# Two-bank PSUM tiles at the end of batch 0, and a later start of batch 1's last DFT, in a fused FFT-mixing and MLP kernel

## The chip, the cores and the metric

The kernel runs on one core of a Trainium2 chip. The metric is the time of one execution on the device in microseconds. The kernel before takes 848.44 us (median of 3 runs, 848.11 to 849.39). The granted clock of TensorE (the share of its full speed that it is let run at) is given.

## The reference

For each of 8 batches of 3008 x 256 values: an FFT along the sequence, a complex 256 x 256 product with bias, a soft threshold, the inverse FFT; then a two-layer MLP with a squared ReLU over all 24064 rows.

```python
X = np.fft.rfft(x, axis=1)
Yr = Xr @ w_r - Xi @ w_i + b_r          # and Yi likewise
Yr = np.sign(Yr) * np.maximum(np.abs(Yr) - 0.01, 0.0)
y  = np.fft.irfft(Yr + 1j * Yi, n=3008, axis=1)

r = np.maximum(y @ w_in, 0.0)           # 256 -> 2048, "hidden"
out = (s * (r * r) + b) @ w_out         # 2048 -> 256, "output"
```

As `(s*r*r + b) @ w_out = s*(r*r) @ w_out + b * colsum(w_out)`, the kernel computes the column sum of w_out once.

## The kernel before

The FFT of length 3008 = 94 x 32 is done in steps: an input DFT over 94 (result `u`), a forward DFT over 32, the mixing product, an inverse DFT over 32 (`v`), and a last DFT over 94 (result `yt`). Batch 0 keeps all of this on the chip; its `v` is turned by identity matmuls (`vt` to `vs`). Later batches go through DRAM (`ud`, `vd`), and their pieces are spread over slots of the MLP's main loop. A slot is one chunk `mc` of hidden units; there are 16 to a tile of up to 512 columns.

The kernel uses eight banks of PSUM, the memory that matmuls write to. `psa` (`other_bank`) and `psf` (`one_bank`) have two each. The other four are `psm` during batch 0 and then `psh`, two tiles of two banks, for the hidden matmuls.

```python
def any_bank():                       # batch 0's tail rotates through all eight
    turn_of[0] += 1
    if "h" in pools:
        return (other_bank, one_bank)[turn_of[0] % 2]()
    return (mix_bank, one_bank, mix_bank, other_bank)[turn_of[0] % 4]()

def turn(ec, k):                      # in first_batch()
    for i in range(2):
        ps = any_bank() if ec else mix_bank()
        ...                           # 4 matmuls into the bank
        evac(vs[...], ps[0:96]..., 512)

def last_dft(ec, n2):
    if ec or n2 >= 16:
        ps = [any_bank(), any_bank()]
    else:
        ps = [one_bank(), other_bank()]
    ...                               # 8 matmuls, 4 into each bank
    for i in range(2):
        evac(yt[...], ps[i][:, 0:384]..., 384)
...
for k in range(4):
    turn(1, k)
    some(1)                           # one unit of batch 1's input DFT
    if k:
        last_dft(1, 8 * (k - 1))
last_dft(1, 24)
```

`evac` gives a PSUM tile to ScalarE or VectorE, whichever has less estimated load. The column sum of w_out is made by GpSimd (`sum_w_out`, eight adds), then spread over the partitions by one matmul of ones, planned for slot 15:

```python
def make_bias():
    ps = other_bank()
    nc.tensor.matmul(ps[:, 0:D], ones, w_sum, start=True, stop=True)
    for j in range(2):
        nc.scalar.activation(out=bias_bc[:, j], in_=ps[:, 0:D], func=AF.Copy, scale=bb_bc)
...
schedule(0, 10, more)
plan.setdefault(15, []).append(make_bias)
...
schedule(mark[1] - 14, 12, s4_units(1))   # batch 1's last DFT: 14 units over 12 slots
```

The order in which the program is written is not the order on the engines: the framework's scheduler lays the instructions out per engine when the program is built. An engine's list is then worked off in order: in the changed kernel, below, TensorE stands 1.53 us before one matmul while ready ones are next in its list.

## Time and profile before

| what | value |
|---|---|
| time | 848.44 us; span in the profile 846.2 us |
| TensorE, VectorE, ScalarE busy | 99%, 82%, 76% |
| first hidden matmul, first ReLU of the MLP | 47.94 us, 49.14 us |
| 6th, 41st, 49th ReLU of the MLP | 54.56, 129.73, 147.74 us |
| batch 1's last DFT | begins at 130.88 us |

The starts of the MLP's ReLUs are used below as milestones: there are 384 in every version, so the n-th in one trace answers to the n-th in another, and the difference of their starts tells how late one kernel is at that point.

### The profile page before, as it was taken

Reading aid. Unit: us, or ns where it says so; the run is one execution under the profiler, and the core shown is the slowest. Engines: PE = TensorE matmul, PEld = TensorE weight load, DVE = VectorE, ACT = ScalarE, POOL = GpSimd, SP = SyncE. Lnnn points to the kernel's source line nnn. Section 1 sums busy time; section 2 is a strip of 40 time slices with the busy share of each in tenths; the row PEclk is TensorE's granted clock in tenths of the full one; section 3 lists DMA queues with packets and bytes.
Section 4 is the critical chain, followed back from the end, with each engine's and each line's share of the span. In section 5 each row is a group of like instructions: output and inputs, shape, how many; then the busy total and the mean of one; then the engine's idle time right before and its main releaser. Section 6 shows DMA issues by size and latency. Waiting matters only on the chain.

```text
span 846.2 us, 17115 instructions
## 1 busy us (share of the span) xinstructions
PE 833.9 (99%) x6653; PEld 599.6 (71%) x6653; DVE 691.8 (82%) x1026; ACT 642.7 (76%) x864; POOL 46.0 (5%) x71
## 2 busy tenths in 40 slices
PE   8999999999999999999999999999999999999997
PEld 6857766777677766777677776777667777766765
DVE  5989987888878987888888888798977888776674
ACT  5988886787778787788777887788877778666673
POOL 4341000000000001000000000000000000000000
PEclk9999999999999999999999999999999999999999
DMA  8945568224762367324761247613354223411111
GB/s 201 181 142 122 122 151 212 67 72 103 173 185 57 99 169 182 96 75 108 189 170 51 78 102 199 171 41 91 101 156 122 62 78 97 112 33 38 38 44 50
DMA packets 105747, 96.06 MB, mean 114 GB/s; under 512 B 9543, under 2 KB 97483, under 8 KB 104323
## 3 DMA queue, kind: packets, MB, share of 16 engines
q1 hardware_dynamic: 99218, 80.55, 32.9%
q0 software_dynamic: 6448, 14.42, 10.7%
q8 instruction: 52, 0.85, 0.4%
q14 instruction: 29, 0.23, 0.1%
HBM read 53.52 MB, written 46.66 MB: 118 GB/s over the span
## 4 chain that ended last, share of the span: by engine, by line
PE 89%; DVE 4%; DMA 3%; ACT 3%; issue 1%; POOL 0%; DVEq 0%; ACTq 0%; SPq 0%; POOLq 0%
PE psa L840 36%; PE psh L769 36%; PE psf L635 4%; PE psf L570 2%; PE psf L621 2%; PE psf L606 2%; PE psf L718 2%; PE psf L665 2%; ACT rt L776 1%; DVE gt L783 1%; DMA vd<-v 1%; PE psm L426 1%; DMA vs<-vd 1%; DMA x<-in_x_dram 1%; DMA F_c<-dft_fwd 0%
## 5 line engine op out<-in xcount | busy, mean ns | idle before, releaser
L776 ACT ACTIVATE rt<-psh 128x1024 f32<-128x1024 f32 (+2 forms) x384 | 386.8, 1009 | 119.6 <-PE psh L769 117.8
L783 DVE TENSOR_TENSOR gt<-rt 128x1024 f16<-128x1024 f32 (+2 forms) x321 | 383.9, 1199 | 98.3 <-ACT rt L776 97.6
L840 PE MATMUL psa<-w_out_t,gt 128*128 128x256 f16 (+1 forms) x3024 | 454.6, 272 | 0.1
L840 PEld LDWEIGHTS <-gt 128*128 128x128 f16 (+1 forms) x3024 | 301.0, 101 | 187.0 <-issue 1.4
L769 PE MATMUL psh<-yt,w_in 128*128 128x512 f16 (+1 forms) x1344 | 396.3, 378 | 0.2 <-ACT rt L776 0.2
L769 PEld LDWEIGHTS <-w_in 128*128 128x128 f16 x1536 | 142.9, 98 | 28.0 <-issue 2.0
L850 DVE SCALAR_TENSOR_TENSOR ost<-psa,s_bc,bias_bc 128x512 f32<-128x512 f32 (+2 forms) x97 | 71.0, 732 | 8.3 <-PE psa L840 6.7
L780 ACT ACTIVATE gt<-rt 128x1024 f16<-128x1024 f32 (+2 forms) x63 | 66.2, 1050 | 1.0
L640 DVE TENSOR_TENSOR ring<-psf,s 128x512 f16<-128x512 f32 x84 | 57.4, 684 | 3.7 <-PE psf L635 3.1
L170 ACT CAST v<-psf 128x512 f16<-128x512 f32 x78 | 45.3, 582 | 18.7 <-PE psf L665 18.7
L170 ACT CAST xf<-psf 128x512 f16<-128x512 f32 x82 | 47.9, 585 | 10.9 <-PE psf L606 10.8
L769 PE MATMUL psh<-tail,w_in 128*128 128x512 f16 (+1 forms) x192 | 52.1, 353 | 0.0
L170 ACT CAST u<-psf 96x512 f16<-96x512 f32 x75 | 43.4, 580 | 10.9 <-PE psf L570 10.7
L635 PE MATMUL psf<-W_g,xf 128*128 128x256 f16 x336 | 50.4, 272 | 0.0
L170 ACT CAST yt<-psf 128x480 f16<-128x480 f32 (+2 forms) x73 | 37.3, 523 | 14.2 <-PE psf L718 14.2
L213 POOL DMA_DIRECT2D x<-in_x_dram x36 | 18.7, 526 | 432.4 <-PE psf L570 431.2
L570 PE MATMUL psf<-x,A_t 94*96 94x512 f16 x103 | 39.3, 381 | 1.7 <-ACT yt L170 0.5
L646 DVE TENSOR_TENSOR ring<-ring,high 128x512 f16<-128x512 f16 x84 | 35.5, 423 | 2.3
L647 DVE TENSOR_TENSOR ring<-ring 128x512 f16<-128x512 f16 x84 | 35.4, 422 | 1.9
L645 DVE TENSOR_TENSOR ring<-ring,low 128x512 f16<-128x512 f16 x84 | 35.4, 421 | 1.6
L635 PEld LDWEIGHTS <-xf 128*128 128x128 f16 x336 | 32.9, 98 | 3.9
L718 PE MATMUL psf<-C_t,vs 96*128 96x96 f16 x448 | 33.0, 205 | 0.9 <-DMA vs<-vd 0.8
(97 smaller groups left out, 500.7 us busy)
## 6 DMA issues: line engine op xcount, KB each, us to landing
out_dram<-ost SPq DMA_DIRECT2D x152, 128.0 KB
ud<-u SPq DMA_DIRECT2D x28, 384.0 KB
us<-ud SPq DMA_DIRECT2D x28, 384.0 KB
vd<-v SPq DMA_DIRECT2D x42, 256.0 KB
vs<-vd SPq DMA_DIRECT2D x14, 768.0 KB
x<-in_x_dram POOLq DMA_DIRECT2D x28, 376.0 KB, 6.5
ring<-ring SPq DMA_DIRECT2D x280, 32.0 KB
out_dram<-ost SPq DMA_DIRECT2D x16, 120.0 KB
```

Of the source, the lines that this page charges most:

```text
L170: return None, nc.scalar.copy(out=dst, in_=src)
L570: nc.tensor.matmul(ps[0:96, :], A_t[0:N1, :], x16[(b, c)][0:N1, j * D : (j + 2) * D], start=True, stop=True,)
L635: nc.tensor.matmul(ps[:, r, :], xt[:, 2 - r, dc], W_g[:, dc, r], start=(dc == 0), stop=(dc == DC - 1),)
L640: nc.vector.tensor_tensor(out=t, in0=ps, in1=hold[i // 2][:, i % 2].unsqueeze(1).to_broadcast([P, 2, D]), op=ALU.add,)
L646: nc.vector.tensor_tensor(out=m, in0=m, in1=high, op=ALU.min)
L718: nc.tensor.matmul(ps[:, j * 96 : (j + 1) * 96], vs[(b, h)][:, k, ec * P : (ec + 1) * P], C_t, start=True, stop=True,)
L769: nc.tensor.matmul(o, w_in_t[dc][:, mc * P : (mc + 1) * P], r, start=(dc == 0), stop=(dc == DC - 1),)
L776: nc.scalar.activation(out=rt[:, :, 0:w], in_=ps[:, :, 0:w], func=AF.Relu)
L780: nc.scalar.activation(out=gt[:, :, 0:w], in_=rt[:, :, 0:w], func=AF.Square)
L783: nc.vector.tensor_tensor(out=gt[:, :, 0:w], in0=rt[:, :, 0:w], in1=rt[:, :, 0:w], op=ALU.mult)
L840: nc.tensor.matmul(ps[0:size, h, :], gts[(ti, mc // 2)][:, mc % 2, sub * size : (sub + 1) * size], w_out_t[:, mc, :], start=(mc == 0), sto ...
L850: nc.vector.scalar_tensor_tensor(out=ost[0:size, 0:k], in0=ps[0:size, 0:k], scalar=s_bc[0:size], in1=bias_bc[0:size, 0:k], op0=ALU.mult, o ...
```

## The change

Its intent: the last four turns and six of the eight last DFTs of batch 0 fill a PSUM tile of two banks and are read by one instruction each (10 evacuations for 20); for this psm is closed and psh opened two steps before the end of batch 0's loop. Besides, batch 1's last DFT starts two slots later and is spread over 16 slots, to wait less for its reload and to have one unit to a slot.

```diff
         def turn(ec, k):
+            if ec:
+                ps = two_banks()
+                for j in range(8):
+                    nc.tensor.matmul(ps[0:96, j // 4, (j % 4) * P : (j % 4) * P + P],
+                                     vt[:, ec, 8 * k + j, :], eye_t, start=True, stop=True)
+                evac(vs[...][:, n : n + 8, ...], ps[0:96]..., 1024)
+                return
         def last_dft(ec, n2):
             if ec or n2 >= 16:
-                ps = [any_bank(), any_bank()]
-            else:
-                ps = [one_bank(), other_bank()]
+                two = two_banks()
+                ...                   # the same 8 matmuls
+                evac(yt[...], two[:, :, 0:384]..., 768)
+                return
+            ps = [one_bank(), other_bank()]
...
         for i in range(2 * U + 2):
+            if i == 2 * U:
+                mix_pool.close()
+                pools["h"] = ctx.enter_context(
+                    tc.tile_pool(name="psh", bufs=2, space=bass.MemoryType.PSUM))
...
-    schedule(mark[1] - 14, 12, s4_units(1))
+    schedule(mark[1] - 12, 16, s4_units(1))
```

(The pool psm is opened inside `first_batch`, and psh is no longer opened after it; the turns that stay single take `mix_bank` without a choice.)

More of the change, by code (lines that the diff above doesn't have):

```diff
@@ L363, in first_batch @@
     def first_batch():
+        mix_pool = ExitStack()
+        pools["m"] = mix_pool.enter_context(
+            tc.tile_pool(name="psm", bufs=4, space=bass.MemoryType.PSUM)
+        )
         ut = ypool.tile([P, DC, 96, N2], F16, name="ut", tag="yt")
@@ L486, in turn @@
         def turn(ec, k):
+            if ec:
+                ps = two_banks()
+                for j in range(8):
+                    nc.tensor.matmul(
+                        ps[0:96, j // 4, (j % 4) * P : (j % 4) * P + P],
+                        vt[:, ec, 8 * k + j, :], eye_t, start=True, stop=True,
+                    )
+                h, n = divmod(8 * k, HW)
+                evac(
+                    vs[(0, h)][:, n : n + 8, ec * P : (ec + 1) * P],
+                    ps[0:96].rearrange("p h (j e) -> p (h j) e", e=P), 1024,
+                )
+                return
             for i in range(2):
-                ps = any_bank() if ec else mix_bank()
+                ps = mix_bank()
                 n = 8 * k + 4 * i
@@ L505, in last_dft @@
             if ec or n2 >= 16:
-                ps = [any_bank(), any_bank()]
-            else:
-                ps = [one_bank(), other_bank()]
+                two = two_banks()
+                for j in range(8):
+                    h, k = divmod(n2 + j, HW)
+                    nc.tensor.matmul(
+                        two[:, j // 4, (j % 4) * 96 : (j % 4) * 96 + 96],
+                        vs[(0, h)][:, k, ec * P : (ec + 1) * P], C_t,
+                        start=True, stop=True,
+                    )
+                evac(
+                    yt[:, ec, n2 : n2 + 8, :].rearrange("p (h j) n -> p h j n", h=2),
+                    two[:, :, 0:384].rearrange("p h (j n) -> p h j n", n=96), 768,
+                )
+                return
+            ps = [one_bank(), other_bank()]
             for j in range(8):
@@ L530, in first_batch @@
         for i in range(2 * U + 2):
+            if i == 2 * U:
+                mix_pool.close()
+                pools["h"] = ctx.enter_context(
+                    tc.tile_pool(name="psh", bufs=2, space=bass.MemoryType.PSUM)
+                )
             if i < 2 * U:
@@ L865, in schedule @@
             plan.setdefault(start + (i * span) // len(units), []).append(u)
-    with tc.tile_pool(name="psm", bufs=4, space=bass.MemoryType.PSUM) as pool:
-        pools["m"] = pool
-        more = first_batch()
-    pools["h"] = ctx.enter_context(
-        tc.tile_pool(name="psh", bufs=2, space=bass.MemoryType.PSUM)
-    )
+    more = first_batch()
     load.update(act=0.0, dve=0.0)
```

## The prediction

> **What bounds the kernel now.** I read the page first, then busy time by window, the waits of TensorE, the chain that ended last in two stretches, and the timeline where the two edits act. The page's first part says that TensorE is the bound:
>
> ```profile
> PE 833.9 (99%) x6653; PEld 599.6 (71%) x6653; DVE 691.8 (82%) x1026; ACT 642.7 (76%) x864; POOL 46.0 (5%) x71
> ```
>
> Only 846.2 - 833.9 = 12.3 us of the span have no matmul in flight, and both edits touch short stages, so nothing here can be worth 2% (17 us). The question is what those two stages lose. Windows (stretch, its length, then busy us and count of PE, PEld, DVE, ACT, POOL, then clock, DMA share, GB/s):
>
> ```profile
> 37.40:41.90 4.50, 3.85 (x45) 2.61 (x43) 4.50 (x9) 3.98 (x9) 0.85 (x1) 1.00 0.67 97
> 41.90:46.20 4.30, 3.55 (x56) 2.79 (x54) 4.30 (x9) 4.26 (x10) 3.99 (x5) 1.00 0.60 176
> 46.20:49.14 2.94, 2.61 (x15) 1.31 (x15) 2.20 (x4) 2.00 (x4) 2.78 (x3) 1.00 0.00 0
> ```
>
> This is the end of batch 0, which the first edit rewrites (37.4 is where its last DFT of n2 16 begins, 49.14 the first Relu of the second network). Until 46.2 VectorE has no gap and ScalarE almost none: it is bound by evacuations, not by TensorE. From 46.2 to 49.14 neither is full. The chain that ended last (start, us, what) and the timeline agree:
>
> ```profile
> 39.08 0.93 DVE yt L174 x2
> 40.00 0.60 DVE u L174
> ...
> 44.36 0.49 ACT u L170
> 44.84 0.49 ACT vs L170
> ```
>
> ```profile
> 47.27 0.56 DVE L174 CAST yt<-psm 128x384 f16<-128x384 f32 x1 [0.61 <-PE psm L511]
> 47.73 0.38 PE L570 MATMUL psf<-x,A_t 94*96 94x512 f16 x1 [0.28 <-ACT u L170]
> 47.74 1.27 DVE L174 CAST u<-psa 96x512 f16<-96x512 f32 x2
> 47.80 1.54 PEld L769 LDWEIGHTS <-w_in 128*128 128x128 f16 x8 [0.60 <-POOL acc L344]
> 47.94 1.89 PE L769 MATMUL psh<-yt,w_in 128*128 128x512 f16 x8
> ```
>
> The chain gives the true pace of an evacuation in a full queue (start to start): 0.60 us for 512 columns on VectorE, 0.49 on ScalarE. The timeline shows the hand-over: the last psm bank is read until 47.83, and the first matmul into psh, which takes over the psm banks, starts at 47.94. The second edit's stage, in the chain:
>
> ```profile
> 124.04 6.79 DMA vs<-vd
> 130.84 0.05 issue
> 130.88 0.60 PE psf L718 x10
> ...
> 137.28 0.42 PE psh L769 x2
> 137.70 0.06 issue
> 137.76 0.66 DVE yt L174
> 138.43 0.04 issue
> 138.47 0.37 PE psf L718 x5
> 138.84 0.41 PE psh L769 x2
> ```
>
> Batch 1's last DFT asks for vs about 0.75 us before the reload lands (TensorE's list of waits puts 0.8 us on it, once), and later TensorE stands for a psf bank until a VectorE evacuation ends.
>
> **What the Trainium skill says.** "Perfetto Trace Analysis", section Optimizing Scalar/DVE Operations, puts the overhead of an instruction that reads PSUM at about 125 ns on VectorE and 51 ns on ScalarE, and says that larger operations help a saturated engine, while splitting them can finish work sooner on one that isn't. Here two widths give the overhead: VectorE pitches of 0.60 (512 columns) and 0.465 (384, half of the 0.93 above) have a slope of 1.05 ns per column and leave 0.06 us; ScalarE's 0.49 and 0.38 leave about 0.05. ScalarE agrees with the page; VectorE's is half the page's. "Advanced Engine Details and Errata", section The Read-Write Bubble, says that one instruction may read several PSUM banks; the trace has it (Relu of 128x1024 out of psh, mean 1009 ns). "Perfetto Trace Analysis", section Matmul Optimizations, wants all eight banks in use. The kernel before rotates through all eight singly in this stretch, and the change keeps eight but as two pairs and four singles. "DMA: Bandwidth & Descriptors", section Rules for kernel authors: wait late on a transfer issued early. The trace agrees with its 0.8 us.
>
> **The change part by part.**
>
> *Fewer evacuations.* Six calls of the last DFT and four of the turn had two evacuations each, 20 in all; they get 10. Columns stay the same, so 10 overheads of some 0.055 us go: 0.55 us over two engines that share the work, 0.28 us of time if both stay full.
>
> *Hand-over of the banks.* In the kernel before psh can open only when psm has been read out, as the timeline shows. In the new one psh opens at step 12, in the stream: the first pair of hidden matmuls needs only the psh pair of the next-to-last DFT tile, the second pair that of the last. So hidden matmuls may start while the last tile is still read. From 46.2 to 49.14 there are 2.94 x 2 = 5.9 us of engine time, with 4.2 used: up to 0.8 us per engine to gain.
>
> *Price of pairs.* A pair takes 8 matmuls of some 0.055 us (0.44), some 0.2 us until the evacuation begins, then 0.9 to 1.13 us for 1024 columns (Relu and square in a full queue: 0.92 and 1.13) or 0.7 to 0.87 for 768 (by the slopes), then some 0.1. A cycle is 1.75 or 1.5 us on average. Four turns and four DFTs of the second half through two pairs take (4 x 1.75 + 4 x 1.5) / 2 = 6.5 us. They begin at 41.3 (first turn, which waits for the last vt), so the hidden matmuls come at about 47.6 and the first Relu at about 48.6, against 49.14. Evacuation work in the same time: 4 x 1.02 + 4 x 0.78 + 10 u tiles x 0.54 = 12.6 us, 6.3 per engine: nearly full too, so an u tile in front of a needed pair costs some tenths. I take a gain of 0.5 us for all three together; the formula alone would allow 0.9.
>
> *Last DFT of batch 1, two slots later over 16.* A slot is 0.41 + 0.44 = 0.85 us of hidden and output matmuls; start moves from slot 82 to 84, 1.7 us plus an input-DFT matmul of 0.22. The reload still lands at about 130.85, TensorE asks at about 132: the 0.75 us go. Before, 14 units over 12 slots put two in one slot twice. The first pair of units follows the wait and takes 0.60 us for ten matmuls where two fives take 0.42 (0.21 each in the chain): 0.17 lost. The second pair is the stop at 137.70: 1.14 us until 138.84 where 0.43 would do, 0.71 lost. Over 16 slots each slot has one at most. The other single slots show no loss (0.21 + 0.41 + 0.44 = 1.06 and the pitch is 1.06). So 0.75 + 0.17 + 0.71 = 1.6 us; I take 1.4, since which engine evacuates what shifts. Batch 1's first hidden tile (slot 96) needs n2 0 to 15, whose last unit is then in slot 92, so finishing at slot 98 costs nothing.
>
> Sum: 848.4 - 0.5 - 1.4 = 846.5.
>
> **Rivals.** (1) Pairs starve TensorE: with two psh pairs and in-order queues the chain turn, evacuation, DFT, evacuation gets longer, since one engine now takes 1.0 us where two took 0.6 side by side; u tiles have only psf and psa, which the last inverse DFT uses too. For it: the 6.3 against 6.5 us above leave no room. Against it: turns run one ahead of DFTs, so the latency is mostly covered. It would turn -0.5 into +1: about 848. (2) The delay is given back: u, xf and v work after slot 98 meets the last units, or the reload lands later because the start of the kernel changed. The page's busy shares of VectorE in 130 to 146 (about 75%) speak against it. It would leave -0.7: about 847.2. (3) The first stage's gain is swallowed in the first hidden tile, where no output matmuls lie beside it and ScalarE is busy 10.45 of 10.86 us (49.14 to 60.00): total evacuation work sets its end, so only the 0.28 us and the filled gaps count. About 846.9. (4) Both work in full: -0.9 and -1.6, 845.9.
>
> **Range and chances.** Between (4) with a little luck in the later balance of the two engines and (1) lies 845.0 to 848.3; three runs of before spread over 1.3 us. A move of 17 us either way has nothing to come from: faster 0.01, same 0.98, slower 0.01.
>
> **What would show it.** Right: 10 fewer evacuations in all; first Relu of the second network at about 48.6; no wait of the last DFT's matmuls on vs; no evacuation of yt in the chain in the stretch of batch 1's last DFT. Wrong: TensorE waiting on evacuations of vs between 41 and 48 and a first Relu later than 49.2, or the vs wait still there. The time would also be off if the steady stage after 150 us, which I take as unchanged, moved by over a microsecond.

## More of the kernel before

The profile's lines are shown in the prediction. Two more belong to them, which I had in view and passed over. They are from the timeline (start us, length us, engine, line, operation, out<-in, count):

```profile
49.67 0.72 POOL L345 TENSOR_TENSOR w_sum<-acc 128x256 f16<-128x256 f32 x1
...
51.99 0.27 PE L349 MATMUL psa<-w_sum,ones 128*128 128x256 f16 x1
```

GpSimd ends the column sum at 50.39. The bias matmul that needs it comes at 51.99, behind sixteen hidden matmuls, and waits for nothing.

## The result

The changed kernel takes 851.50 us (median of 6 runs, 851.18 to 853.2) against 848.68 us for the kernel before in the same rounds (847.46 to 850.08). A ratio here and below goes by mean times of runs of the same rounds, so it is not quite the ratio of the medians. It is 1.0036, with a 95% interval of 1.0023 to 1.0050: slower, by a sixth of the 2% that would count as slower. The prediction of 846.5, range 845.0 to 848.3, was wrong, and in sign.

The profiled run takes 851.18 us, with a span of 849.2 us against 846.2. The page's first line has the ten missing evacuations (VectorE 1026 to 1021, ScalarE 864 to 859), and nothing else of note:

```profile
PE 836.7 (99%) x6653; PEld 601.8 (71%) x6653; DVE 693.5 (82%) x1021; ACT 642.7 (76%) x859; POOL 48.1 (6%) x71
```

The milestones say where the time came from. The first ReLU of the MLP starts at 52.95 us against 49.14; the 17th at 79.41 against 75.25, so 4.16 late; the 41st at 133.89 against 129.73, still 4.16; the 49th at 150.53 against 147.74, 2.79 late. Some 4.2 us are lost before the second tile, 1.37 are won in the stretch of batch 1's last DFT, and nearly nothing moves after that.

The chain that ended last (followed back from the last instruction, at each step to what released it; start, us, what), for the changed kernel where the loss arises:

```profile
47.53 1.16 POOL acc L344
48.70 0.07 issue
48.76 1.17 POOL acc L344
49.93 0.07 issue
50.00 0.73 POOL w_sum L345
50.73 0.04 issue
50.77 0.37 PE psa L349
51.14 3.24 PE psh L802 x8
```

Where the chain of before has evacuations, this one holds GpSimd's adds for the column sum of w_out, and then the bias matmul. The timeline of TensorE shows the same from its side:

```profile
48.73 0.51 PE L526 MATMUL psh<-C_t,vs 96*128 96x96 f16 x8 [0.82 <-ACT vs L170]
...
50.77 0.37 PE L349 MATMUL psa<-w_sum,ones 128*128 128x256 f16 x1 [1.53 <-POOL w_sum L345]
```

The bias matmul (L349) now stands **in front of** the hidden matmuls in TensorE's list, and TensorE stands 1.53 us until the sum is there. The first hidden matmul starts at 50.94 instead of 47.94. And it doesn't run at full pace: eight hidden matmuls take 3.24 us in the chain, 0.405 each, where the chain of before has 1.94 us for eight, at most 0.24 each. Windows (stretch, length, busy us and count of PE, PEld, DVE, ACT, POOL, then granted clock, DMA share, GB/s) show why. Before:

```profile
47.00:50.70 3.70, 3.26 (x19) 1.44 (x17) 2.25 (x4) 3.19 (x5) 3.16 (x4) 1.00 0.35 102
50.70:52.00 1.30, 1.30 (x8) 0.53 (x7) 1.30 (x2) 1.30 (x3) 0.00 (x0) 1.00 0.03 13
52.00:54.50 2.50, 2.46 (x15) 1.29 (x14) 2.50 (x3) 2.50 (x4) 0.00 (x0) 1.00 0.53 157
```

After:

```profile
47.00:50.70 3.70, 1.33 (x17) 0.77 (x17) 2.04 (x3) 2.86 (x5) 3.46 (x4) 0.99 0.37 110
50.70:52.00 1.30, 1.23 (x4) 0.55 (x4) 0.00 (x0) 0.82 (x2) 0.02 (x1) 0.50 0.93 268
52.00:54.50 2.50, 2.50 (x8) 0.91 (x7) 0.50 (x1) 1.14 (x3) 0.00 (x0) 0.59 0.12 35
```

After a stretch of 3.70 us in which TensorE was busy for only 1.33, its granted clock is 0.50 and then 0.59, and the PE column reads 95 and 100% busy on half as many matmuls.

One thing more lies in the traces' clock records, and it explains oddities below. The granted clock changes only at the ends of equal stretches of 3.41 us, whose place differs from run to run. In the changed kernel's run the half clock fills one such stretch, 50.63 to 54.05; in those of experiments 3, 4 and 6 it fills two (6.83 us). Cut along these stretches, TensorE is busy in the one before the fall for 1.11 us (stretch, length, PE alone, clock, DMA share, GB/s):

```profile
47.22:50.63 3.41, 1.11 (x15) 1.00 0.39 115
50.63:54.05 3.42, 3.28 (x9) 0.50 0.39 115
```

Another stretch of this run, 9.67 to 13.09, has the half clock too. So a run's mean granted clock alone doesn't say where clock was lost.

The second part did what it was made for. The chain after, in the stretch of batch 1's last DFT, has neither the DMA nor the evacuation of `yt`; single groups of five matmuls lie between hidden and output matmuls:

```profile
138.09 0.44 PE psa L873 x4
138.53 0.21 PE psf L751 x5
138.74 0.41 PE psh L802 x2
139.15 0.44 PE psa L873 x4
```

So the theory: **the pairs of banks did not slow the evacuations much; they changed the order on TensorE, so that a matmul with a late operand came to stand in front of work that was ready, and the idleness that followed cost the clock as well.** The rivals: that pairs starve TensorE by themselves (the prediction's first rival); that a wait of ScalarE for a `u` buffer, seen below, is the cause; and that the clock fell for a reason of its own.

### The profile page after: what moved, and what is told of

Same layout as the page of the kernel before. It is cut to its first block, busy times and chain, and to the rows that moved or that the text cites. A ratio compares the mean times of both kernels' runs of the same rounds, so it can differ in the third digit from the quotient of the medians.

```text
span 849.2 us, 17102 instructions
## 1 busy us (share of the span) xinstructions
PE 836.7 (99%) x6653; PEld 601.8 (71%) x6653; DVE 693.5 (82%) x1021; ACT 642.7 (76%) x859; POOL 48.1 (6%) x71
## 4 chain that ended last, share of the span: by engine, by line
PE 90%; DMA 4%; ACT 2%; POOL 2%; issue 1%; DVE 1%; SPq 0%; DVEq 0%; ACTq 0%; POOLq 0%
PE psh L802 37%; PE psa L873 37%; PE psf L668 4%; PE psf L603 2%; DMA w_out_t<-in_moe_w_out_dram 2%; PE psf L654 2%; PE psf L639 2%; PE psf L698 2%; PE psf L751 2%; ACT rt L809 1%; POOL acc L344 1%; DMA x<-in_x_dram 1%; POOL x L213 0%; DMA F_t<-fwd_rest 0%; DVE gt L816 0%
## 5 line engine op out<-in xcount | busy, mean ns | idle before, releaser
L802 PE MATMUL psh<-yt,w_in 128*128 128x512 f16 (+1 forms) x1344 | 398.0, 379 | 0.3 <-ACT rt L809 0.2
L802 PEld LDWEIGHTS <-w_in 128*128 128x128 f16 x1536 | 143.3, 98 | 29.3 <-issue 4.7
L813 ACT ACTIVATE gt<-rt 128x1024 f16<-128x1024 f32 (+2 forms) x62 | 65.3, 1054 | 1.0
L170 ACT CAST u<-psf 96x512 f16<-96x512 f32 x79 | 45.7, 580 | 13.0 <-PE psf L603 11.7
L802 PE MATMUL psh<-tail,w_in 128*128 128x512 f16 (+1 forms) x192 | 52.1, 353 | 0.0
```

The source lines that it names most:

```text
L170: return None, nc.scalar.copy(out=dst, in_=src)
L802: nc.tensor.matmul(o, w_in_t[dc][:, mc * P : (mc + 1) * P], r, start=(dc == 0), stop=(dc == DC - 1),)
L813: nc.scalar.activation(out=gt[:, :, 0:w], in_=rt[:, :, 0:w], func=AF.Square)
```

## The experiments

Twelve kernels ran, all with correct results, five or six runs each. The kernel before had, in the rounds, medians of 848.12 (first four), 848.36 (next four) and 848.05 us (last four). Lines of the kernel files shift between versions: the hidden matmul is L769 before, L802 after, L773 or L813 below.

### 1. The change with the bias matmul held behind the hidden ones

```diff
-    plan.setdefault(15, []).append(make_bias)
+    def late_bias():
+        with tc.issue_after(hidden[(0, 7)].ins):   # the 16th hidden matmul
+            make_bias()
+    plan.setdefault(15, []).append(late_bias)
```

`issue_after` only orders the list of the engine; it is no wait.

> The changed kernel with one edge added: the bias matmul (the column sum of w_out) may be issued only after the 16th hidden matmul, where it stood before. My theory, that this matmul at the head of TensorE's queue holds the hidden matmuls back until GpSimd's sum is ready and that the idle time then halves the granted clock, expects the first Relu of the second network at about 50.5 us instead of 52.95, a clock of 1.00 between 50.7 and 54.5 instead of 0.50 to 0.59, and a time of some 848.6 us, level with the kernel before. The rival, that the pairs of banks alone starve TensorE, expects no change: 851.5 us and a low clock still.

Measured: 848.08 us (848.01 to 848.93), ratio 1.0000 (0.9988 to 1.0011). The loss against before is gone with one edge of order. (It is not at 0.9987, where experiment 2 is; see experiment 9.) The first ReLU comes at 49.26, earlier than I expected, and the 6th at 54.55, level with before (54.56). The clock stays:

```profile
47.00:50.70 3.70, 3.12 (x22) 1.39 (x20) 2.09 (x4) 3.02 (x5) 3.46 (x4) 1.00 0.66 196
50.70:52.00 1.30, 1.30 (x8) 0.58 (x6) 1.30 (x2) 1.05 (x2) 0.09 (x1) 1.00 0.13 47
```

### 2. The kernel before with the second edit alone

```diff
-    schedule(mark[1] - 14, 12, s4_units(1))
+    schedule(mark[1] - 12, 16, s4_units(1))
```

> The kernel before with the second edit alone (batch 1's last DFT from two slots later, over 16 slots). The traces of before and after differ by 1.4 us less after this stage than ahead of it, so if that is this edit's doing it gives 847.3 us, 0.9984 of before, and no wait of the last DFT on vs. The rival, that the reload only came in time because the changed kernel was late at its start, expects the wait still there and no gain: 848.7.

Measured: 847.33 us (846.87 to 847.83), ratio 0.9987 (0.9974 to 1.0000). TensorE has no wait on `vs` in its list. Against before, this kernel is 0.63 us late at the 41st ReLU (130.36) and 0.74 early at the 49th (147.00): the edit wins 1.37 us there, in a run that was not late by a stall.

### 3. The change with its first part alone

The edit of experiment 2 the other way round, on the changed kernel.

> The change with its first part alone (pairs of banks; batch 1's last DFT as before). If the two parts add up, this is slower than both: 851.5 + 1.4 = 852.9 us, 1.005 of before. If they don't (if the delay at the start hides the wait on vs anyway), 851.5.

Measured: 852.27 us (849.63 to 853.32), ratio 1.0043 (1.0030 to 1.0056). The parts add up: 1.0043 x 0.9987 = 1.0030 for 1.0036 measured. TensorE waits 2.7 us for the column sum in the profiled run, and its first hidden matmul starts at 50.93, as in the changed kernel. One of the six runs took 849.63 us, the others 851.6 to 853.3. That run has a mean granted clock of 1.000, so no half clock anywhere; the others have 0.994 to 0.998, which may be lost elsewhere too (experiment 10's profiled run, at 847.62 us, has 0.998, from a half clock at 9.44 to 12.85 us). It is one run, but it fits: same order, the clock not lost.

### 4. The kernel before with the bias matmul put in front

```diff
-    schedule(0, 10, more)
-    plan.setdefault(15, []).append(make_bias)
+    schedule(0, 1, more)
+    plan[0].append(late)              # make_bias, issued after unit 14 of the input DFT
...
+                    with tc.issue_after(bias_mm[0].ins):
+                        first_mm(ti, mc)           # for the very first hidden matmul
```

> The kernel before, its single banks untouched, with the bias matmul forced ahead of the first hidden matmul (and the last six units of the input DFT asked for together, so that they stay ahead of it). My theory expects TensorE to wait for GpSimd's sum until about 50.5, some 2.5 us, a halved clock for about 3 us after it, and a time of 848.7 + 3.5 to 4 us, so some 852.5, without any pair of banks. The rival (pairs are the cause) expects about 849.

Measured: 852.74 us (852.36 to 854.23), ratio 1.0055 (1.0043 to 1.0067), and there is no pair of banks in it. Its chain:

```profile
49.43 0.73 POOL w_sum L345
50.16 0.04 issue
50.20 0.37 PE psa L349
50.58 5.13 PE psh L773 x12
```

Twelve hidden matmuls in 5.13 us are 0.43 each, half pace. The list of waits names only 0.9 us of wait on the sum, less than the 2.5 I expected; the windows show 2.12 us busy of the 3.70 before 50.7, so the rest lies in other gaps around the last units of the input DFT. The clock falls at 48.75 already, after a stretch of 3.42 us with 1.98 us busy, while the wait for the sum begins only at 49.27: here the half clock comes of those gaps, the last of which, 0.37 us long, the kernel before fills with hidden matmuls. (The edit also puts the last unit, which stood behind eight hidden matmuls, in front of them.) So the loss can be had without the change, by the order alone; that it is the wait for the sum alone, this experiment doesn't show.

### 5. The change with TensorE kept at work while it waits

```diff
+        with tc.issue_after(fill[0].ins), tc.issue_after(unit_mm[-1].ins):
+            for _ in range(28):
+                f = nc.tensor.matmul(ps[:, D : D + P], ones, ones, start=True, stop=True)
+        with tc.issue_after(f.ins):
             nc.tensor.matmul(ps[:, 0:D], ones, w_sum, start=True, stop=True)
```

(`fill[0]` is the last matmul of the last DFT. The first hidden matmul is ordered behind the bias, which is where the changed kernel has it; the built order is otherwise the same.)

> The changed kernel in its own order, but with 28 matmuls of ones (written to the unused half of the bias bank, some 1.5 us of work) put right before the bias matmul, so that TensorE works while GpSimd finishes its sum. The wait for the sum stays (first hidden matmul still at about 50.9), only the idleness goes. If the idleness is what halves the clock, the clock stays at or near 1.00 after it and the time falls by 1.5 to 2.7 us, to 849 to 850. If the clock falls for another reason, or costs nothing, it stays at 851.5.

Measured: 850.32 us (850.04 to 851.33), ratio 1.0025 (1.0012 to 1.0037): just above what I expected. The clock holds, though the wait is there (0.98 us are left of it behind the filling, and the first hidden matmul starts at 52.04, as GpSimd's sum is late in this run, at 51.88):

```profile
47.00:50.70 3.70, 3.23 (x52) 2.65 (x52) 3.39 (x5) 2.52 (x4) 3.46 (x4) 1.00 0.49 152
50.70:52.00 1.30, 0.32 (x6) 0.20 (x4) 0.00 (x0) 0.00 (x0) 1.10 (x2) 1.00 0.83 246
52.00:54.50 2.50, 2.19 (x11) 0.95 (x11) 0.28 (x1) 2.17 (x4) 0.00 (x0) 1.00 0.09 30
```

So the idleness is what halves the clock. (This is one profiled run, the slowest of the five. Its sum is late, and its mean clock 0.996, because its half clock lies at 9.49 to 16.32 us, at the start of the kernel.) From the first hidden matmul to the 6th ReLU the traces have 6.62 us before, 7.73 after, 8.29 in experiment 3, 8.47 in experiment 4, 8.59 in experiment 6 and 6.37 here. Against this run, which has the same order at full clock, the half clock costs 1.4 us in the changed kernel and 1.9 and 2.2 in experiments 3 and 6. The median gained less, 0.0036 - 0.0025, or some 0.9 us, from ratios of different rounds.

### 6. The change with smaller u buffers

In the changed kernel ScalarE stands 1.10 us before an evacuation of `u`, while the last turn's tile waits behind it:

```profile
46.70 1.06 ACT L170 CAST u<-psf 96x512 f16<-96x512 f32 x2 [1.10 <-PE psh L494]
47.66 1.02 ACT L170 CAST vs<-psh 96x1024 f16<-96x1024 f32 x1
```

The profile puts this down to TensorE. The program says otherwise: that instruction waits for several semaphores, a DMA's among them, since the fourth `u` tile takes the buffer of the first, whose store must have landed. In the run of experiment 9 the profile names it:

```profile
46.27 1.07 ACT L170 CAST u<-psf 96x512 f16<-96x512 f32 x2 [0.94 <-DMA ud<-u]
```

```diff
-    upool = ... tc.tile_pool(name="up", bufs=3)
+    upool = ... tc.tile_pool(name="up", bufs=6)
...
-                hold["u"] = upool.tile([P, XCH, D], F16, name="u", tag="u")
+                hold["u"] = upool.tile([P, 4, D], F16, name="u", tag="u")
```

(With stores to match. Four buffers of the old size did not fit into SBUF.)

> The changed kernel with the u tiles of the input DFT halved and their number doubled (six of 2 KB instead of three of 4 KB, stores of half the size), so that the last units find a free tile without waiting for the first store to land; order of TensorE and ScalarE unchanged. In the changed kernel's trace ScalarE stood for 1.1 us at 45.6 before such a unit, put down to TensorE. My theory expects that wait to shrink or go and TensorE to end its last DFT about a microsecond earlier, but the hidden matmuls still to start at about 50.9, behind the bias matmul, and the clock to fall as before or longer: 851.5 us or slightly more. The rival, that this wait on a buffer is what delays the hidden matmuls, expects about 850.

Measured: 850.72 us (849.95 to 852.68), ratio 1.0032 (1.0019 to 1.0044). The wait of ScalarE is gone, the last DFT ends on TensorE at 48.49 instead of 49.24, and the hidden matmuls start where they did:

```profile
51.08 0.37 PE L349 MATMUL psa<-w_sum,ones 128*128 128x256 f16 x1 [2.60 <-POOL w_sum L345]
```

What was won went into a longer wait for the sum, 2.60 for 1.53 us. As a cause of the late start of the hidden matmuls this rival falls. The time alone wouldn't decide: 850.72 lies between the 851.5 and the 850 expected, with three runs at 849.95 to 850.72 us (clock 0.998) and two at 852.36 and 852.68 (0.995 and 0.993).

### 7 and 8. Smaller u buffers with the late bias, and with single banks

Experiment 7 is experiment 1 with the edit of 6; experiment 8 is experiment 2 with it.

> Pairs, new schedule, late bias matmul and the halved u tiles together. With the bias out of the way the buffer wait is next: in the run with the late bias alone it was short in the profile, so I expect 847.5 to 848.1 us, at most 0.5 us better than without the halved tiles, and if the pairs are worth anything in themselves a time below the 847.3 us of the new schedule alone.

> Single banks, new schedule, halved u tiles: the candidate for the best version beside the new schedule alone (847.3). I expect the same within 0.5 us: here the last units come after the first store has landed anyway.

Measured: 847.81 us (847.52 to 849.0), ratio 0.9995 (0.9981 to 1.0008) for 7; 847.43 us (846.92 to 848.19), ratio 0.9989 (0.9976 to 1.0001) for 8. With pairs the smaller buffers may give some 0.05%, within the intervals; with single banks nothing. Pairs do not go below the new schedule alone.

### 9. The pairs alone, with the bias matmul held behind

Experiment 1 with the old schedule: what the first part is worth if the order is kept.

> The pairs alone: late bias matmul, batch 1's last DFT on the old schedule. It measures what my prediction put at -0.5 us. From the two profiles with the late bias and with the new schedule alone, which run level after the first tile, I expect 848.4 us, the same as before within 0.4 us; if the prediction's term was right after all, 847.9 and below; if pairs cost something of themselves, 849 and above.

Measured: 848.77 us (848.56 to 851.22), ratio 1.0009 (0.9997 to 1.0022). The expected gain of 0.5 us is not there; a loss of about that size is more likely than a gain. Two other pairs of kernels of the same rounds differ by the pairs and the held order alone and say the same: by mean times experiment 1 is 0.93 us above experiment 2, with a standard error of 0.23 us from the runs' spread, and 7 is 0.54 above 8 (0.33); here it is 0.74 above before (0.47). So with the order held the pairs seem to cost 0.5 to 0.9 us. By what is not shown. In the profiled run the buffer wait of experiment 6 shows (0.94 us), and the first hidden matmul starts at 49.00, against 48.14 in experiment 1.

### 10, 11 and 12. Pairs in one part only, and one pair less

Before these I built three versions with fewer pairs, and looked at TensorE's list: in each the bias matmul stands behind twenty hidden matmuls, with no edge asked for. Of these versions, only the one with all the pairs has it in front. (The order differs in more than that: of the sixteen units of the input DFT, ten, thirteen and eleven stand before the first hidden matmul in 10, 11 and 12; in the changed kernel all sixteen do.)

```diff
-            if ec or n2 >= 16:                          # 10: the turn alone in pairs
+            if False:
-            if ec:                                      # 11: the last DFT alone in pairs
+            if False:
-            if ec or n2 >= 16:                          # 12: all but the last tile in pairs
+            if (ec or n2 >= 16) and (ec, n2) != (1, 24):
```

(In 10 and 11 the other part takes single banks from `any_bank`, as before.)

> The changed kernel with pairs in the turn alone (the last DFT in single banks). Built, its order on TensorE has the bias matmul behind 20 hidden matmuls without any edge asked for. So no stall and no halved clock: with the new schedule about 847.4 to 848.1 us. If pairs in the turn are harmful whatever the order, 849 or more.

> The changed kernel with pairs in the last DFT alone (the turn in single banks). Its order, too, has the bias matmul behind 20 hidden matmuls. Expected: no stall, clock 1.00, 847.4 to 848.1 us; 849 or more if pairs in the last DFT are harmful in themselves.

> The changed kernel with one tile less in a pair: the last of the last DFT (second half of e, n2 24) takes two single banks again. Its order has the bias matmul behind 20 hidden matmuls. If the order is the cause, taking this one pair back takes the whole loss away: 847.4 to 848.1 us, some 3.5 us under the change. If the number of pairs is the cause, it saves a tenth: about 851.

Measured: 847.64 us (847.59 to 848.14), ratio 0.9992 (0.9980 to 1.0004); 847.70 us (847.31 to 848.51), ratio 0.9993 (0.9981 to 1.0005); 848.39 us (848.1 to 850.05), ratio 1.0002 (0.9990 to 1.0014). One tile of ten back in single banks takes nearly the whole loss away, so most of it is the order, not the number of pairs. Twelve is a little above what I expected, though, and its profiled run is its slowest, at 850.05 us, with a half clock and no long wait:

```profile
44.00:47.00 3.00, 2.01 (x32) 1.69 (x33) 3.00 (x4) 1.39 (x4) 2.83 (x3) 1.00 0.48 143
47.00:48.50 1.50, 1.03 (x17) 0.84 (x17) 0.22 (x2) 1.50 (x2) 1.42 (x2) 0.94 0.01 3
48.50:51.00 2.50, 2.50 (x8) 0.94 (x6) 1.09 (x2) 1.05 (x3) 2.34 (x3) 0.50 0.00 0
```

The longest single wait of TensorE ahead of it is 0.45 us; the gaps add up to 1.0 of 3.0 us and 0.5 of 1.5 us. They are waits for evacuations of `vs` and `yt` (0.45, 0.41, 0.34, 0.26 and 0.22 us), which is what the prediction's first rival describes: in this execution pairs did starve TensorE enough to lose the clock. Its four other runs (848.1 to 848.5 us) don't show the loss in their times. Such a stage is close to the edge from one execution to the next, as the stretches of 3.41 us fall differently. Here is the one before the fall, and the least busy one of this stage that still kept the clock, from experiment 2 (PE alone):

```profile
44.92:48.33 3.41, 1.97 (x33) 1.62 (x33) 2.15 (x3) 1.80 (x3) 3.17 (x4) 1.00 0.39 117
48.33:51.75 3.42, 3.42 (x13) 1.32 (x11) 1.24 (x2) 1.81 (x4) 3.19 (x4) 0.50 0.00 0
```

```profile
44.64:48.05 3.41, 2.34 (x26) 1.00 0.33 97
```

In the fourteen traces, the clock fell in this stage after stretches with 1.11 (the change), 1.47, 1.97, 1.98 and 2.19 us busy (experiments 6, 12, 4 and 3), and it stayed at full after every stretch with 2.34 or more. Where between them the line lies, and whether it is a line, these runs don't show.

### The best version

The new schedule alone (experiment 2) is the best measured, 847.33 us, ratio 0.9987, with an interval that just reaches 1. Experiments 8, 10 and 11 (0.9989 to 0.9993) are not told apart from it, and it is the smallest edit.

## Why the prediction was wrong

**Bound, first stage.** The reading that evacuations bound the end of batch 0 was right as far as it went; that stage stays evacuation-bound with the order kept (in experiment 1 VectorE has no gap from 42.14 to 47.74 us, and ScalarE none from 42.58 to 48.57).

**Fewer evacuations, hand-over, price of pairs: here is the step that failed, the hand-over.** The prediction put the three together at -0.5 us, from "the hidden matmuls come at about 47.6 and the first Relu at about 48.6". They came at 50.94 and 52.95. The term measured +0.0043 of 848 us, some 3.6 us, where I had -0.5. The step assumed that a hidden matmul starts when its banks are free. It left out the list: what stands before it on the engine must be ready too. I had the bias matmul at 51.99 and the sum's end at 50.39 in the traces, and did not ask what would happen if the scheduler, seeing other banks free, placed it elsewhere. Putting it back takes 1.0043 (experiment 3) to 1.0009 (experiment 9), 2.9 of the 3.6 us; putting it in front without the change (experiment 4) makes a loss, and one pair less (experiment 12), with another order, does nearly without it. In the changed kernel's trace, 4.12 us late at the 6th ReLU, 1.1 to 1.4 us are the halved clock (against 6.62 us before and 6.37 in experiment 5), and the rest is mostly the start of the hidden matmuls, which is bound to the end of the sum at 50.72.

**What the pairs are worth in themselves** was also mis-sized. With the order held, they measure 1.0009 (experiment 9), which by itself doesn't tell a small loss from none and leaves no room for the 0.5 us; with the two other comparisons a loss of 0.5 to 0.9 us is likelier. The hidden matmuls come at 48.14 then (experiment 1), not at 47.6. The prediction's own sum, 41.3 + 6.5, gives 47.8 where it writes 47.6. The ten overheads did go. What took their place in some runs is a wait I had not listed: the evacuations of `u` come earlier relative to their stores, and ScalarE stands for a buffer whose store hasn't landed.

**The rivals.** Rival 1 named the direction, and the sign it had written for itself, TensorE waiting on evacuations of `vs`, is there (0.82 us). It is not the cause: experiment 6 takes the wait in front of it away and the hidden matmuls start no earlier. But in one execution of experiment 12 it was at work, without the bias matmul. Rival 2 is not seen: the changed kernel is 2.79 us late at the 49th ReLU and 2.91 at the last. Rival 3 was not tested.

**The second part was right**, in mechanism and size: -1.4 predicted, 1.37 between the 41st and 49th ReLU, both with the pairs and without. The wait for `vs` is gone and the evacuation of `yt` is out of the chain. Over the whole kernel the edit alone gives 1 - 0.9987, 1.1 us.

**What stays open** is why the scheduler placed the bias matmul first. Of the versions built, it does so only with all the pairs. That the hidden matmuls' banks look taken at that point by the last two DFT tiles, and that its estimate has GpSimd's sum ready too early, is my guess and was not tested.

## What to carry to other kernels

Before moving buffers in a scheduled program, list the instructions with late operands near the place, and after building compare the order on the bounding engine; where such an instruction must not lead, give it an edge of order, which brought 851.50 us to 848.08 here. A stall or a row of gaps of one or two microseconds on TensorE can cost about as much again in granted clock (1.53 us of wait and 1.4 us here), so read the clock in the windows after a wait, not only the wait. A wait that the profile puts down to an engine that had long been done can be a buffer's earlier store.

## What the Trainium skill lacked or had wrong

- "TensorE: Matmul & The Clock Gate", sections What's actually happening and HAM oscillation: the page has the clock halved after an idle window of about 3.4 us and gives as the rule no gaps above that. The stretches of 3.41 us are in the traces, but one need not be idle: it was enough that TensorE was busy for 1.11 to 2.19 us of it, and 2.34 us were enough to keep the clock (at the end of batch 0; at the start of the kernel a stretch with 58% busy was followed by the half clock in experiment 5 and not in experiment 3, so no threshold comes out). Gaps far below the rule did it: one wait of 1.53 us with 0.82 us ahead of it (1.33 us busy in 3.70), and in one run of experiment 12 only gaps of up to 0.45 us (2.01 busy of 3.00, then 1.03 of 1.50). The same page's section A second HAM failure mode: psum-queue depth-cycling does tell of short but frequent idle times between groups of matmuls, so it is the rule that falls short. That it varies from run to run, as the page says of a free-running window, agrees with experiment 3 (one run of 849.63 us at clock 1.000 beside five at 851.6 to 853.3). Its half rate agrees: 0.43 us for a matmul of 512 columns in experiment 4, against 0.22 at full clock (four in 0.88 us in experiment 5's chain).
- "Perfetto Trace Analysis", section Optimizing Scalar/DVE Operations: the overhead of VectorE on PSUM is given as about 125 ns; in a full queue two widths leave about 0.06 us, as the prediction works out. The changed kernel's wider reads lie on the same line: start to start, VectorE takes 0.86 us for 768 columns and 1.13 for 1024, ScalarE 0.69 and 0.91. ScalarE's 51 ns agrees.
- No page that I found says that the placing of an instruction by a scheduler can change when only buffers change, or to look for it: the bias matmul moved from behind 16 hidden matmuls to the front, and the ratio is 1.0036 with it there and 1.0000 with it held back (experiment 1).
